# Two edits to the transfers of a fused sparse attention and MoE kernel: the overlap copies of v as SBUF-to-SBUF transfers, and q and k loaded a row ahead

## The chip, the cores and the metric

The kernel runs on one core of a Trainium2 chip. The metric is the time of one execution on the device, in microseconds; where several runs are given, their median. A core has five engines that follow their own instruction queues and wait for each other by semaphores: TensorE (PE; its weight loads are listed as PEld), VectorE (DVE), ScalarE (ACT), GpSimd (POOL) and SyncE (SP). Transfers are issued by SyncE and by GpSimd here, each with a queue of its own (q1 and q0 in the profile), and carried by sixteen DMA engines.

## The reference

Attention over a batch of 8 rows, 8 heads, 576 positions and 64 features. Heads 0 to 3 see a sliding window of 32 positions, heads 4 to 7 a dilated one of 32 positions with a step of 4. The result, laid out by token (4608 x 512), goes through an MLP with a squared ReLU.

```python
mask_plain = (rel >= 0) & (rel < window)
mask_dil = (rel >= 0) & (rel < window * dilation) & (rel % dilation == 0)
scores = np.where(masks[None, :, :, :], scores, -1000000000.0)
attn = np.exp(scores - np.max(scores, axis=-1, keepdims=True))
attn = attn / (np.sum(attn, axis=-1, keepdims=True) + 1e-09)
x = np.matmul(attn, v).transpose(0, 2, 1, 3).reshape(B * S, H * D)

h = x @ w_in                # 512 -> 2048
r = np.maximum(h, 0.0)
out = (r * r) @ w_out       # 2048 -> 512
```

## The kernel before, in words

The attention goes by batch rows `b` of 576 tokens, the MLP by nine chunks `c` of 512 tokens. A stage is one row `b` with chunk `b - 1` beside it: the chunk's code is a generator, and `pump(n)` between pieces of attention lets it emit `n` more pieces. The order of instructions on every engine is thus the order in which the program emits them; each engine takes its own in order. Chunks 2 and up form the second product by a Strassen scheme of seven half-size products that accumulate in three PSUM banks, `pa`, `pb` and `pc` (`mm2_strassen_gen`, L348). ScalarE evicts `pa` (`take`, L386) before the next product may add to it.

What a row of attention needs, and how it comes:

- q and k of the sliding heads: GpSimd's queue loads them with a cast to half precision (`ns`, L112); VectorE copies them into token order (`nr`, `by_token`, L120); SyncE's queue stores that to DRAM (`dp`, L211) and reads it back transposed (`QKTp`, L219).
- q and k of the dilated heads: GpSimd's queue copies them, cast, within DRAM (`dd`, L201); SyncE's queue reads them transposed (`QKTd`, L223).
- v: SyncE loads it in single precision (`sv`, L132; `sd`, L137), GpSimd casts it (`vp`, L169; `vd`, L177). The windows of neighbouring blocks overlap, so the last 32 partitions of one block of `vp` are also the first 32 of the next, and the upper 64 partitions of `vd`'s first half are the lower 64 of its second. ScalarE makes these overlap copies: three `halo_sliding` (L184) and two `halo_dilated` (L189) a row.

In the stage, scores (`ps`, `pz`) go through ScalarE's exponential and VectorE's mask (L546, L547), the weighted sums (`pav`, `paw`) are normalised by VectorE (`xs`, `xd`, L593). From row 4 on, SyncE's queue transposes these into `xT` directly for the sliding heads (L663) and into `yd` for the dilated ones (L670), and ScalarE copies `yd` into `xT` (`x_from`, L658). `xT` feeds the next chunk's first product (`ph`, L293), which ScalarE evicts (`rt`, L316) and VectorE squares (`g`, L317).

Order of the transfers in a stage `b` of 4 to 6: GpSimd first copies one element of the last `QKTd` into `seen` (L230), that is, it waits until the transposes for row `b` have landed; then it issues `ns` and `dd` for row `b + 1`. After the scores VectorE makes `nr`, and SyncE issues `dp`, `sv`, the `xs` transposes, `QKTp`, the two `yd`, `QKTd`, `sd`, and last the chunk's output. A tile of the pool `natp` has two buffers, taken in turn by `ns` and `nr`, so `ns` of the next row may come once `nr` has been made from the last.

The three lines that the prediction's steps turn on:

```python
hooks[3] = turn                          # L851: nr, dp, sv for the next row, after the scores
attn_values_by_dma(b, (turned, done))    # L863: turned: QKTp; done: QKTd, sd, seen, vp
x_from(b, 0, ys[0])                      # L732: ScalarE's copy of the first yd
```

Of the kernel before, what the change touches and what calls it, by code (L numbers as in the profile page):

```python
# [13 lines left out]
P = 128  # L14
# [3 lines left out]
def kernel(  # L18
# [9 lines left out]
    nc = tc.nc  # L28

    B, H, S, D = q.shape  # L30
# [16 lines left out]
    NB = S // QB  # L47
    PADP = P - QB
# [33 lines left out]
    HF = NFF // 2  # L82
# [26 lines left out]
    def load_sliding_qk(b):  # L109
        n = natp.tile([P, HH, 9 * D], FP16, name=f"ns{b}", tag="n")  # L110
        for i, s in ((1, k), (0, q)):
            nc.gpsimd.dma_start(  # L112
                out=n[64 * i : 64 * (i + 1)],
                in_=s[b, 0:HH].rearrange("h (p j) d -> p h (j d)", j=9),
            )
        return n

    def by_token(b, n):
        r = natp.tile([P, 9, HH, D], FP16, name=f"nr{b}", tag="n")
        (nc.gpsimd if b == 2 else nc.vector).tensor_copy(  # L120
            r.rearrange("x j h d -> x h j d"), n.rearrange("x h (j d) -> x h j d", d=D)
        )
        return r
# [49 lines left out]
    def cast_dilated_v(b):  # L173
        for t in range(2):
            p0 = 64 * t
            for c in range(0, DIL, 2):
                nc.gpsimd.tensor_copy(  # L177
                    vd[b % 2][p0:P, t, c : c + 2, :, 0:D],
                    sd[p0:P, t, :, D * c : D * (c + 2)].rearrange("p h (c d) -> p c h d", d=D),
                )  # L180

    def halo_sliding(b, mp):
        m0, m1 = max(1, 2 * mp), 2 * mp + 2
        nc.scalar.copy(  # L184
            vp[b % 2][0:PADP, m0:m1, :, 0:D], vp[b % 2][P - PADP : P, m0 - 1 : m1 - 1, :, 0:D]
        )

    def halo_dilated(b, c):
        nc.scalar.copy(  # L189
            vd[b % 2][0:64, 1, c : c + 2, :, 0:D], vd[b % 2][64:P, 0, c : c + 2, :, 0:D]  # L190
        )

    def cast_v(b):
        cast_sliding_v(b)
        cast_dilated_v(b)


    def keep_dilated_qk(b):
        d = dpool.tile([2, HH * CL, DIL * D], FP16, name=f"dd{b}", tag="dd")
        for i, src in ((1, k), (0, q)):  # L200
            nc.gpsimd.dma_start(  # L201
                out=d[i].rearrange("(r i) x -> r (i x)", i=4),
                in_=src[b, HH:H].rearrange("h (r i) d -> (h r) (i d)", i=16),
                max_dma_last_dim=4096,
            )
        return d

    def keep_sliding_qk(b, r):
        d = dpool.tile([2, S, HH * D], FP16, name=f"dp{b}", tag="dp")
        for i in (1, 0):  # L210
            nc.sync.dma_start(  # L211
                out=d[i].rearrange("(p j) x -> p (j x)", j=9),
                in_=r[64 * i : 64 * (i + 1)].rearrange("p j h d -> p (j h d)"),
            )
        return d
# [12 lines left out]
    def after_transposes(b):  # L228
        t = QKTp[b % 2][:, 0, 1, PADP : PADP + 1] if b == 2 else QKTd[b % 2][:, 0, 1, KPAD : KPAD + 1]
        nc.gpsimd.tensor_copy(seen, t)  # L230
# [9 lines left out]
    for r in range(2):  # L240
        nc.vector.memset(QKTp[r][:, 1, :, 0:PADP], 0.0)
        nc.vector.memset(QKTd[r][:, 1, :, 0:KPAD], 0.0)
        nc.vector.memset(vp[r][:, :, :, D : D + 1], 1.0)
        nc.vector.memset(vp[r][0:PADP, 0, :, D : D + 1], 0.0)
        nc.vector.memset(vd[r][:, 1, :, :, D : D + 1], 1.0)
    nc.vector.memset(AT[:, :, UW:640], 0.0)
    reli = const.tile([P, QB], I16, name="reli")
    nc.gpsimd.iota(reli, pattern=[[1, QB]], base=0, channel_multiplier=-1)
# [58 lines left out]
    def mm1_gen(c, g, sums=False, begun=()):  # L307
        for ffc in range(NFF):
            if ffc < len(begun):
                ph = begun[ffc]  # L310
            else:
                ph = mm1_begin(c, ffc)
                yield
            mm1_half(c, ffc, ph, (2, 3))
            rt = osb.tile([P, TOKC], FP16, name=f"rt{c}_{ffc}", tag="rt")
            nc.scalar.activation(rt, ph[:], ACTF.Relu)  # L316
            nc.vector.tensor_mul(g[:, ffc, :], rt, rt)  # L317
            if c == 1 and ffc % 2 == 0:
                next(w_sums)
            if sums and ffc % 4 == 3 and ffc >= HF:  # L320
                sum_of_g(g, ffc - 3, ffc + 1)
            yield

    def sum_of_g(g, f0, f1):
        k = slice(f0 - HF, f1 - HF)
        nc.vector.tensor_add(gs[0][:, k], g[:, k, HTOK:], g[:, f0:f1, HTOK:])
        nc.vector.tensor_sub(gs[1][:, k], gs[0][:, k], g[:, k, 0:HTOK])  # L327
# [167 lines left out]
    def pump(n):  # L495
        for _ in range(n):
            while pending:
                try:
                    next(pending[0])
                    break  # L500
                except StopIteration:
                    pending.pop(0)
# [152 lines left out]
    def x_from(b, t, y):  # L655
        t0 = b * S % XW + DIL * Q0D[t]
        o = xT[:, 2:4, t0 : t0 + DIL * QD[t]].rearrange("x c (i r) -> x c i r", r=DIL)
        nc.scalar.copy(o, y.rearrange("x r c i -> x c i r"))  # L658
# [16 lines left out]
    def attn_scores(b, gap, less=0, hooks={}):  # L675
        for hp in range(2):
            s_sliding(b, hp)
            if hp in hooks:
                hooks[hp]()
            pump(gap)  # L680
        for g in range(2):
            s_dilated(b, g)
            if 2 + g in hooks:
                hooks[2 + g]()
            if g and b < 4:
                halo_sliding(b, 0)
            pump(gap - less)

    def attn_values(b, gap, wide=False, hooks={}):
        xs = x_tiles(b)  # L690
        for mp in range(3):
            av_sliding(b, mp, xs)
            if mp < 2:
                halo_sliding(b, mp + 1)
            else:
                halo_dilated(b, 0)
            pump(gap)
        x_sliding(b, 0, xs, wide)
        halo_dilated(b, 2)
        pump(gap)  # L700
        av_dilated(b, 0, 0, xs)
        pump(gap)
        x_sliding(b, 1, xs, wide)
        pump(gap)
        av_dilated(b, 0, 1, xs)
        pump(gap)
        for a in range(2):
            av_dilated(b, 1, a, xs)
            pump(gap)
        x_dilated(b, 0, xs, wide)  # L710
        pump(gap)
        x_dilated(b, 1, xs, wide)

    def attn_values_by_dma(b, then):
        xs = x_tiles(b)
        for mp in range(3):
            av_sliding(b, mp, xs)
            if mp:
                halo_dilated(b, 2 * mp - 2)
            pump(3)  # L720
        x_sliding_by_dma(b, xs)
        ys = []
        for t in range(2):
            for a in range(2):
                av_dilated(b, t, a, xs)
                pump(4 + 2 * (a > t))
            if t == 0:
                then[0]()
            ys.append(x_dilated_by_dma(b, t, xs))
        then[1](ys[1])  # L730
        pump(6)
        x_from(b, 0, ys[0])  # L732
        pump(7)
        x_from(b, 1, ys[1])

# [79 lines left out]
    load_v(2)  # L815


    for b in range(2, B):
        pending.append(moe_gen(b - 1))
        nxt = b + 1  # L820
        hooks = {}
        if nxt < B:
            after_transposes(b)
            ns = load_sliding_qk(nxt)
            if b == 2:
                cast_v(b)
            dd = keep_dilated_qk(nxt)
        if b > 4:
            cast_dilated_v(b)
        if b > 3:  # L830
            hooks.update({n: lambda n=n: halo_sliding(b, n + 1) for n in range(2)})
        kept = []

        def turn():
            kept.append(keep_sliding_qk(nxt, by_token(nxt, ns)))
            load_sliding_v(nxt)

        def turned():
            if nxt < B:
                transpose_sliding(nxt, kept[0])  # L840

        def done(y):
            if nxt < B:
                transpose_dilated(nxt, dd)
                if b > 3:
                    load_dilated_v(nxt, nc.sync)
                    nc.gpsimd.tensor_copy(seen, y[:, 0, 0, 0:1])
                    cast_sliding_v(nxt)

        if nxt < B:  # L850
            hooks[3] = turn  # L851
        if b > 3:
            halo_sliding(b, 0)
        pump({2: 24, 3: 16}.get(b, 3))
        attn_scores(b, 4 if b == 2 else 3, 0, hooks)
        if b < 4:
            load_dilated_v(nxt, nc.sync)
            turned()
            done(None)
            cast_v(nxt)  # L860
            attn_values(b, b)
        else:
            attn_values_by_dma(b, (turned, done))  # L863
        pump(1000)
    pending.append(moe_gen(B - 1))
    pending.append(moe_gen(B))
# [31 lines left out]
```

The softmax here doesn't subtract the row's maximum and nothing guards it: scores larger than these inputs give would overflow.

## Time and profile before

| | us |
|---|---|
| median of 11 runs | 307.75 |
| lowest and highest of them | 306.95 and 310.22 |
| the profiled execution | 310.15 |
| its span, first to last instruction | 307.8 |

The profile is of one execution; its span leaves out what lies before the first and after the last instruction, 2.35 us. When transfers were issued and when they landed, in row 4 (the stage from 128.76 to 159.30 us), from the trace:

| transfer | queue | issued | landed |
|---|---|---|---|
| QKTd for row 4, second | SyncE | 126.64 | 130.51 |
| ns for row 5, k and q | GpSimd | 131.21, 131.85 | 137.39, 138.38 |
| dd for row 5, k and q | GpSimd | 132.45, 133.00 | 139.78, 141.20 |
| dp for row 5, two | SyncE | 139.30, 139.87 | 142.84, 144.13 |
| sv for row 5, two | SyncE | 140.55, 141.34 | 145.80, 147.03 |
| xT from xs, two | SyncE | 143.15, 144.91 | 147.55, 149.39 |
| QKTp for row 5, two | SyncE | 146.29, 147.63 | 150.54, 151.69 |
| yd, first and second | SyncE | 149.72, 152.53 | 152.60, 155.17 |
| QKTd for row 5, two | SyncE | 153.83, 155.18 | 157.76, 158.91 |

The rows of a timeline are read as start, length, engine, line, operation and tiles; the bracket at the end tells how long the engine was idle before it and what released it. The DMA row of the page gives the mean busy share of the sixteen DMA engines in 40 equal slices, in tenths.

### The profile page before, as it was taken

What the parts mean: (1) busy time and instruction counts of PE and PEld (TensorE: products, weight loads), DVE (VectorE), ACT (ScalarE), POOL (GpSimd) and SP (SyncE); (2) the same over time, 40 slices, a digit from 0 to 9 for tenths busy, and PEclk for the clock granted to TensorE, in tenths of its full rate; (3) what the DMA queues carried; (4) which work ended last, traced back from release to release, by engine and by line L of the source; (5) the groups of instructions that cost most, each with busy time, mean ns of one, the idle gap of its engine ahead of it and who ended that gap; (6) DMA issues with size and microseconds to landing.
All of it is one profiled execution on the core that took longest, in us unless ns stands there. A gap on an engine that the chain in (4) does not pass through costs nothing.

```text
span 307.8 us, 6916 instructions
## 1 busy us (share of the span) xinstructions
PE 289.7 (94%) x2762; PEld 193.4 (63%) x2762; DVE 208.8 (68%) x433; ACT 184.9 (60%) x318; POOL 67.7 (22%) x117
## 2 busy tenths in 40 slices
PE   1988998997999999999999999999999999999994
PEld 1545554553455558745888997458745875785583
DVE  7774448666962698579939993899389934834652
ACT  2766648666835893597459736963597446425620
POOL 4481008411804401430054004500230000000000
PEclk9999999999999999999999999999999999999999
DMA  7899997899799989999899999989943230003004
GB/s 119 187 196 214 206 170 112 159 214 225 121 206 214 212 161 195 217 200 192 133 195 254 175 137 201 238 166 140 169 140 24 44 116 34 2 1 139 0 0 136
DMA packets 76751, 45.92 MB, mean 149 GB/s; under 512 B 58352, under 2 KB 69104, under 8 KB 76720
## 3 DMA queue, kind: packets, MB, share of 16 engines
q1 hardware_dynamic: 67648, 30.81, 49.7%
q0 software_dynamic: 9072, 14.68, 27.2%
q8 instruction: 21, 0.34, 0.5%
q14 instruction: 10, 0.08, 0.1%
HBM read 36.70 MB, written 16.52 MB: 173 GB/s over the span
## 4 chain that ended last, share of the span: by engine, by line
PE 71%; DMA 8%; DVE 8%; ACT 6%; issue 3%; SPq 2%; POOL 0%; DVEq 0%; POOLq 0%
PE ph L293 27%; PE pa L370 15%; PE pb L370 7%; PE po L436 7%; DMA ns<-in_q_dram 5%; PE pc L370 4%; ACT AT L546 4%; PE paw L621 3%; ACT rt L316 2%; DVE AT L547 2%; PE pav L605 2%; DMA QKTd<-dd 2%; PE pf L490 2%; DMA QKTp<-dp 1%; DVE xs L593 1%
## 5 line engine op out<-in xcount | busy, mean ns | idle before, releaser
L293 PE MATMUL ph<-xT,wi 128*128 128x512 f16 (+1 forms) x640 | 134.0, 359 | 0.7 <-ACT xT L658 0.7
L316 ACT ACTIVATE rt<-ph 128x512 f16<-128x512 f32 x144 | 84.5, 595 | 37.0 <-PE ph L293 35.7
L293 PEld LDWEIGHTS <-wi 128*128 128x128 f16 x640 | 68.2, 114 | 46.1 <-issue 0.6
L317 DVE TENSOR_TENSOR g<-rt 128x512 f16<-128x512 f16 x144 | 61.9, 441 | 39.8 <-ACT rt L316 39.0
L370 PEld LDWEIGHTS <-g 128*128 128x128 f16 x448 | 43.3, 98 | 6.1
L370 PEld LDWEIGHTS <-gs 128*128 128x128 f16 x336 | 32.1, 98 | 4.1 <-DVE gs L327 0.5
L436 PE MATMUL po<-wo,g 128*128 128x512 f16 x128 | 33.1, 380 | 0.0
L397 DVE TENSOR_TENSOR ov<-pb,ov 128x512 f32<-128x512 f32 x14 | 9.7, 691 | 31.0 <-PE pb L370 17.4
L370 PE MATMUL pa<-wt,gs 128*128 128x256 f16 x224 | 27.3, 273 | 0.0
L370 PE MATMUL pb<-wt,g 128*128 128x256 f16 x224 | 27.1, 273 | 0.0
L169 POOL CAST vp<-sv 128x512 f16<-128x512 f32 x24 | 14.4, 633 | 51.7 <-DMA sv<-in_v_dram 51.7
L177 POOL CAST vd<-sd 128x512 f16<-128x512 f32 (+1 forms) x32 | 22.5, 732 | 9.1 <-PE ps L556 5.4
L386 ACT COPY ov<-pa 128x512 f32<-128x512 f32 x14 | 8.2, 586 | 27.0 <-PE pa L370 26.9
L547 DVE TENSOR_TENSOR AT<-AT,maskp 128x576 f16<-128x576 f16 x32 | 19.5, 626 | 6.2 <-ACT AT L546 5.0
L593 DVE TENSOR_TENSOR xd<-paw,rcp_d 80x512 f16<-80x512 f32 (+1 forms) x32 | 21.9, 685 | 1.1
L546 ACT ACTIVATE AT<-ps 128x576 f16<-128x576 f32 x32 | 18.9, 644 | 2.7 <-PE ps L556 2.2
L546 ACT ACTIVATE AT<-pz 128x576 f16<-128x576 f32 x32 | 19.0, 652 | 1.8 <-PE pz L575 1.7
L386 ACT COPY ou<-pa 128x512 f32<-128x512 f32 x14 | 8.2, 586 | 16.0 <-PE pa L370 16.0
L593 DVE TENSOR_TENSOR xs<-pav,rcp_p 96x512 f16<-96x512 f32 x24 | 16.5, 687 | 0.8
L547 DVE TENSOR_TENSOR AT<-AT,maskd 128x576 f16<-128x576 f16 x32 | 15.4, 506 | 2.1 <-ACT AT L546 0.8
L621 PEld LDWEIGHTS <-AT 128*128 128x128 f16 x256 | 11.9, 98 | 5.6 <-PE paw L621 1.3
L436 PEld LDWEIGHTS <-g 128*128 128x128 f16 x128 | 10.3, 97 | 8.1
(83 smaller groups left out, 295.2 us busy)
## 6 DMA issues: line engine op xcount, KB each, us to landing
sv<-in_v_dram SPq DMA_DIRECT2D x14, 288.0 KB, 5.7
dp<-nr SPq DMA_DIRECT2D x12, 288.0 KB, 4.2
out_dram<-ou SPq DMA_DIRECT2D x6, 512.0 KB, 4.8
out_dram<-ov SPq DMA_DIRECT2D x6, 512.0 KB, 4.4
sd<-in_v_dram SPq DMA_DIRECT2D x8, 320.0 KB, 5.8
ns<-in_k_dram POOLq DMA_DIRECT2D x8, 288.0 KB, 6.5
ns<-in_q_dram POOLq DMA_DIRECT2D x8, 288.0 KB, 7.1
sd<-in_v_dram SPq DMA_DIRECT2D x8, 256.0 KB, 6.1
```

The source lines that it names most:

```text
L169: nc.gpsimd.tensor_copy(vp[b % 2][:, m : m + 2, :, 0:D], sv[:, :, m : m + 2, :].rearrange("p h m d -> p m h d"))
L177: nc.gpsimd.tensor_copy(vd[b % 2][p0:P, t, c : c + 2, :, 0:D], sd[p0:P, t, :, D * c : D * (c + 2)].rearrange("p h (c d) -> p c h d", d=D),)
L293: nc.tensor.matmul(ph[:, t0:t1], wi4[ffc // 4][:, dmk, :, ffc % 4], xT[:, dmk, x0 : x0 + t1 - t0], start=(dmk == 0 and t0 == 0), stop=(dmk ...
L316: nc.scalar.activation(rt, ph[:], ACTF.Relu)
L317: nc.vector.tensor_mul(g[:, ffc, :], rt, rt)
L370: nc.tensor.matmul(banks[bank][:, t], a(k, t), b(k), start=(new and t == 0 and k == 0), stop=(k == HF - 1), skip_group_check=True,)
L386: nc.scalar.copy(ot, banks[A])
L436: nc.tensor.matmul(po, g[:, ffc, t * P : (t + 1) * P], wo[ffc // 4][:, ffc % 4, :], start=(ffc == 0), stop=(ffc == NFF - 1),)
L546: nc.scalar.activation(AT[:, u, 0:UW], ps[:, :, 0 : UW // 2], ACTF.Exp, scale=scale)
L547: nc.vector.tensor_mul(AT[:, u, 0:UW], AT[:, u, 0:UW], mask)
L593: nc.vector.tensor_tensor(out=x, in0=pv, in1=rb, op=ALU.mult)
L621: nc.tensor.matmul(pav[:, e, h * (D + 2) : h * (D + 2) + D + 1], AT[:, 4 + h, off : off + P], vd[b % 2][:, t, 2 * a + e, h, 0 : D + 1], st ...
```

## The change

There are two edits. The first: for rows 3 to 7 the overlap of v is copied by one transfer for `vp` and one for `vd` on SyncE's queue, whole rows with the columns that hold ones, in place of ScalarE's five copies; the memsets set both spare columns for this. The second: q and k of row 5 are asked for in row 3's stage, those of row 6 in row 4's after the scores, those of row 7 in row 5's, behind `cast_dilated_v`. For rows 6 and 7 the token-order copy and `dp` stand in the Strassen part of the stage two before, after `x_from` of the first `yd`, together with the overlap of `vp` for the row between. Their `QKTp` and `QKTd` stand at the start of the stage before, followed on SyncE's queue by the overlap of `vd` for that stage's own row and by the load of `sv`. Row 5's token-order copy and transposes stay where they were. The waits by `seen` on `QKTd` go from row 4 on. In chunk 2 the first pair of sums of `g` moves from block 11 to block 13.

```diff
+    def halo_sliding_by_dma(b):
+        nc.sync.dma_start(out=vp[b % 2][0:PADP, 1:NB], in_=vp[b % 2][P - PADP : P, 0 : NB - 1])
+
+    def halo_dilated_by_dma(b):
+        nc.sync.dma_start(out=vd[b % 2][0:64, 1], in_=vd[b % 2][64:P, 0])
...
-        nc.vector.memset(vp[r][:, :, :, D : D + 1], 1.0)
+        nc.vector.memset(vp[r][:, :, :, D : D + 2], 1.0)
         nc.vector.memset(vp[r][0:PADP, 0, :, D : D + 1], 0.0)
-        nc.vector.memset(vd[r][:, 1, :, :, D : D + 1], 1.0)
+        nc.vector.memset(vd[r][:, :, :, :, D : D + 2], 1.0)
...
-            if sums and ffc % 4 == 3 and ffc >= HF:
-                sum_of_g(g, ffc - 3, ffc + 1)
+            if sums and ffc in (13 if c == 2 else 11, 15):
+                f0 = min(ffc // 4 * 4, 12) if ffc != 13 else 8
+                sum_of_g(g, f0, f0 + 4)
...
-            if g and b < 4:
+            if g and b < 3:
                 halo_sliding(b, 0)
...
-            if mp:
-                halo_dilated(b, 2 * mp - 2)
             pump(3)
...
         x_from(b, 0, ys[0])
+        then[2]()
         pump(7)
         x_from(b, 1, ys[1])
```

The loop over the rows, after the change:

```python
    def ask(b):
        if b < B:
            nss[b] = load_sliding_qk(b)
            dds[b] = keep_dilated_qk(b)

    def turn(b):
        if b < B:
            dps[b] = keep_sliding_qk(b, by_token(b, nss[b]))

    for b in range(2, 4):
        ...
        attn_scores(b, 4 if b == 2 else 3, 0, {3: turn_and_load})
        load_dilated_v(nxt, nc.sync)
        transpose_sliding(nxt, dps[nxt])
        transpose_dilated(nxt, dds[nxt])
        cast_v(nxt)
        halo_sliding_by_dma(nxt)
        halo_dilated_by_dma(nxt)
        if b == 3:
            ask(5)
        attn_values(b, b)
        pump(1000)

    for b in range(4, B):
        pending.append(moe_gen(b - 1))
        nxt = b + 1
        hooks = {}
        if b > 4:
            if nxt < B:
                transpose_sliding(nxt, dps[nxt])
                transpose_dilated(nxt, dds[nxt])
            cast_dilated_v(b)
            halo_dilated_by_dma(b)
            if nxt < B:
                load_sliding_v(nxt)
            ask(nxt + 1)
        else:

            def turn_and_load():
                turn(nxt)
                load_sliding_v(nxt)
                ask(nxt + 1)

            hooks[3] = turn_and_load

        def turned():
            if b == 4:
                transpose_sliding(nxt, dps[nxt])

        def done(y):
            if b == 4:
                transpose_dilated(nxt, dds[nxt])
            if nxt < B:
                load_dilated_v(nxt, nc.sync)
                nc.gpsimd.tensor_copy(seen, y[:, 0, 0, 0:1])
                cast_sliding_v(nxt)

        def ahead():
            turn(nxt + 1)
            if nxt < B:
                halo_sliding_by_dma(nxt)

        pump(3)
        attn_scores(b, 3, 0, hooks)
        attn_values_by_dma(b, (turned, done, ahead))
        pump(1000)
```

More of the change, by code (lines that the diff above doesn't have):

```diff
@@ L692, in attn_values @@
             av_sliding(b, mp, xs)
[L693 to L696, printed above, removed]
+            if b < 3:
+                if mp < 2:
+                    halo_sliding(b, mp + 1)
+                else:
+                    halo_dilated(b, 0)
             pump(gap)
         x_sliding(b, 0, xs, wide)
-        halo_dilated(b, 2)
+        if b < 3:
+            halo_dilated(b, 2)
         pump(gap)
@@ L815 @@
     load_v(2)
-    for b in range(2, B):
+    nss, dds, dps = {}, {}, {}
+    def ask(b):
[6 more added lines that the diff above has]
+    for b in range(2, 4):
+        pending.append(moe_gen(b - 1))
+        nxt = b + 1
+        after_transposes(b)
+        nss[nxt] = load_sliding_qk(nxt)
+        if b == 2:
+            cast_v(b)
+        dds[nxt] = keep_dilated_qk(nxt)
+        def turn_and_load():
+            turn(nxt)
+            load_sliding_v(nxt)
+        pump(24 if b == 2 else 16)
+        attn_scores(b, 4 if b == 2 else 3, 0, {3: turn_and_load})
+        load_dilated_v(nxt, nc.sync)
+        transpose_sliding(nxt, dps[nxt])
+        transpose_dilated(nxt, dds[nxt])
+        cast_v(nxt)
+        halo_sliding_by_dma(nxt)
+        halo_dilated_by_dma(nxt)
+        if b == 3:
+            ask(5)
+        attn_values(b, b)
+        pump(1000)
+    for b in range(4, B):
         pending.append(moe_gen(b - 1))
@@ L821, with turn_and_load, done @@
         hooks = {}
[L822 to L827, printed above, removed]
         if b > 4:
+            if nxt < B:
+                transpose_sliding(nxt, dps[nxt])
+                transpose_dilated(nxt, dds[nxt])
             cast_dilated_v(b)
[L830 to L836, printed above, removed]
-        def turned():
-            if nxt < B:
-                transpose_sliding(nxt, kept[0])
-        def done(y):
-            if nxt < B:
[L844 to L863, printed above, removed]
+            halo_dilated_by_dma(b)
+            if nxt < B:
+                load_sliding_v(nxt)
+            ask(nxt + 1)
+        else:
+            def turn_and_load():
+                turn(nxt)
+                load_sliding_v(nxt)
+                ask(nxt + 1)
+            hooks[3] = turn_and_load
+        def turned():
+            if b == 4:
+                transpose_sliding(nxt, dps[nxt])
+        def done(y):
+            if b == 4:
+                transpose_dilated(nxt, dds[nxt])
+            if nxt < B:
+                load_dilated_v(nxt, nc.sync)
+                nc.gpsimd.tensor_copy(seen, y[:, 0, 0, 0:1])
+                cast_sliding_v(nxt)
+        def ahead():
+            turn(nxt + 1)
+            if nxt < B:
+                halo_sliding_by_dma(nxt)
+        pump(3)
+        attn_scores(b, 3, 0, hooks)
+        attn_values_by_dma(b, (turned, done, ahead))
         pump(1000)
```

## The prediction

> **What bounds the kernel now.** I read the page first, then the busy time by stage, then the matrix engine's and ScalarE's own rows in those stages, and last the transfers by queue. The page:
>
> ```profile
> span 307.8 us, 6916 instructions
> PE 289.7 (94%) x2762; PEld 193.4 (63%) x2762; DVE 208.8 (68%) x433; ACT 184.9 (60%) x318; POOL 67.7 (22%) x117
> DMA  7899997899799989999899999989943230003004
> ```
>
> TensorE is busy for 289.7 of 307.8 us; a gain can only come out of the other 18.1. The last row shows the sixteen DMA engines nearly full from the second slice to the thirtieth. By stage (a stage is the time of one attention row with the MoE chunk beside it; rows 3, 4, 5, 6, 7, then the first chunk alone; columns are length, PE, PEld, DVE, ACT, POOL, clock, DMA share, GB/s):
>
> ```profile
> 97.00:128.76 31.76, 31.39 (x317) 21.60 (x315) 22.85 (x47) 21.19 (x39) 9.59 (x16) 1.00 1.04 187
> 128.76:159.30 30.54, 30.22 (x291) 20.96 (x290) 22.86 (x49) 20.38 (x36) 4.66 (x10) 1.00 0.96 185
> 159.30:189.50 30.20, 29.91 (x351) 27.27 (x350) 23.99 (x48) 20.29 (x35) 7.13 (x12) 1.00 0.99 188
> 189.50:221.20 31.70, 30.81 (x293) 20.95 (x292) 23.98 (x49) 20.35 (x35) 7.32 (x13) 1.00 0.97 184
> 221.20:251.60 30.40, 30.08 (x289) 20.86 (x288) 23.28 (x47) 19.88 (x34) 2.83 (x4) 1.00 0.35 71
> 251.60:277.70 26.10, 26.10 (x178) 18.18 (x176) 13.73 (x25) 11.90 (x20) 0.00 (x0) 1.00 0.12 44
> ```
>
> TensorE idles 0.37, 0.32, 0.29, 0.89 and 0.32 us in rows 3 to 7, 2.19 together. The rest of its 18.1 lies at the start, in rows 0 to 2 and behind the last product, where the change does next to nothing. Two stalls show what the 2.19 is made of:
>
> ```profile
> 134.08 0.31 PE L575 MATMUL pz<-QKTd 64*128 64x80 f16 x8 [0.23 <-ACT AT L546]
> 202.63 0.42 PE L605 MATMUL pav<-vp,AT 128*128 128x65 f16 x8 [0.57 <-DVE xs L593]
> ```
>
> The first waits for ScalarE, full there (the overlap copies of v among its work), and recurs in rows 5 to 7. The second is row 6's: VectorE stood 0.87 us for q's load before the token-order copy, and the normalisation queued behind it. So the stages have little to give, and DMA is 96 to 104% full beside them until row 7. What covers the transfers decides. In row 4:
>
> ```profile
> 132.40:140.00 7.60, 7.28 (x75) 3.86 (x74) 6.23 (x15) 7.32 (x15) 1.16 (x3) 1.00 1.00 157
> 140.00:152.60 12.60, 12.60 (x120) 9.27 (x119) 12.26 (x28) 6.45 (x12) 0.00 (x0) 1.00 1.05 180
> 152.60:154.60 2.00, 2.00 (x20) 1.79 (x19) 1.03 (x1) 1.30 (x1) 0.00 (x0) 1.00 0.35 65
> ...
> 152.63 1.30 ACT L658 COPY xT<-yd 128x640 f16<-128x640 f16 x1 [0.62 <-DMA yd<-xd]
> 154.91 0.59 ACT L386 COPY ov<-pa 128x512 f32<-128x512 f32 x1 [0.99 <-PE pa L370]
> ```
>
> From 132.4 to 140 the load of q and k fills the engines, from 140 to 152.6 the dp store, sv, the xs, QKTp and first yd transposes; only then is there slack. That yd lands at 152.6 and ScalarE already waits 0.62 us for it. Behind the copy stands the eviction of pa at 154.91, and TensorE's next product into pa begins at 155.58: the yd may slip by 0.99 us, and each microsecond more stops TensorE. The queues from 132.4 to 140.2, then from 68.2 to 69 and from 69.2 to 70 (packets, MB, share of 16 engines; q0 is GpSimd's, q1 SyncE's):
>
> ```profile
> q0 software_dynamic: 857, 1.17, 96.5%
> ...
> q0 software_dynamic: 94, 0.32, 98.1%
> q1 hardware_dynamic: 103, 0.02, 13.9%
> ...
> q1 hardware_dynamic: 816, 0.20, 116.5%
> q0 software_dynamic: 15, 0.00, 1.1%
> ```
>
> One load of q and k (ns and dd) takes 7.8 x 0.965 = 7.5 us of all engines. While q0 has work (68.2 to 69), a transpose's 256-byte packets pass one for one with its large ones, 103 against 94; once q0 is empty they run at 816 in 0.8 us, eight times faster.
>
> [...]
>
> **The change part by part.**
>
> *Overlap copies off ScalarE.* 25 copies go (five each for rows 3 to 7): 0.40 + 0.60 + 0.60 + 0.61 + 0.61 = 2.82 us a row, 14.1 us of ScalarE. On the path is only TensorE's idle time: the 0.23 of rows 4 to 7, about 0.1 behind each, and 0.15 of row 3 (pav waiting for vp). Ten transfers are added on SyncE, 84 and 135 KB in rows of 2,640 and 2,112 bytes. No row of before shows an SBUF-to-SBUF copy; the nearest are the sd loads, 0.4 to 0.7 us of issue and 5 us to landing. They wait for GpSimd's casts, done before SyncE gets there (row 4's at 126.3; QKTd's issue ends at 128.0). Behind them on SyncE stand only output stores, and in rows 5 to 7 also sv and xs, at least 5 us early. I take 0, from 0 to +0.5 a row.
>
> *q and k a stage ahead.* Three `seen` copies go (rows 4 to 6), and with them GpSimd's waits of 4.33, 1.83 and 2.89 us that kept the loads behind the transposes. The token-order copy (0.75 us of VectorE) leaves the scores of rows 5 and 6 for the Strassen section, where VectorE has gaps of 1.9 and 2.5 us: the 0.57 of row 6 goes. Moving two 0.69 us sums of chunk 2 from block 11 to 13 may return row 3's 0.21 (xs). Of 2.19 I count 1.9 as won: bounds 1.0 and 2.2. What is late next is the transposes:
>
> (1) Row 4, middle. ns(6) and dd(6) are asked for as soon as VectorE has copied ns(5), about 139. Their 7.5 us fall into 140 to 152.6, which is full, and by turns they go ahead of xs, QKTp and yd. yd: 152.6 + 7.5 = 160.1, less 0.7 (dp no longer stands behind dd(5)'s tail until 140) and about 1 (the two queues overlap, shares of 1.05 to 1.17) = 158.4. Against the limit of 152.6 + 0.99 = 153.6 that is a stall of 4.8 us; 3.5 with transposes at their best rate, 6 at the 600 packets per us that xs to yd averaged.
>
> (2) Row 4, start. ns(5) is asked for behind the casts at 126.3, while QKTd(4) is still moving (landed at 130.51, needed by pz at about 133). If q0's first packet comes 1.2 us later, as at 131.21, QKTd still has about 114 packets an engine, meets all 50 of q0's, and lands at about 137: 3.7 us lost. If it takes 2.9 us, as at 191.17 with engines busy, 28 packets remain and it lands at 133: nothing lost. The engines are busy (1.22), so I take 0.5.
>
> (3) Row 5. ns(7) and dd(7), four transposes and sv now stand before its xs and yd, where ns, dd, dp, sv and two transposes did. Stage and backlog have both slid; yd comes within 0.5 us of its limit. 0 to 2.7, taken as 0.3. Rows 6 and 7 load nothing ahead: 0.
>
> *Edits with one answer.* The wider memsets cost about 0.1 us of VectorE, which is unbroken up to the first QKTp copy at 7.41: +0.1. Moving transposes to the start of rows 5 and 6 costs SyncE only issue time.
>
> Sum: 4.8 + 0.5 + 0.3 + 0.1 - 1.9 = +3.8 us. The profiled span becomes 307.8 + 3.8 = 311.6, its execution 310.15 + 3.8 = 313.95. That execution lies 2.4 above the median of 307.75, so on the median I put 311.5.
>
> **The rivals.** *The covers hold* (the other side, one mechanism): if q0 doesn't take its turns against the transposes beyond row 4's slack, yd lands by 153.6 and only the win is left, 307.75 - 1.8 = 305.9. It decides from where ns(6) and dd(6) delay yd by less than 1 us of their 7.5. For it: q0's packets came up to 2.9 us after issue, so part could slide behind. Against: the one-for-one count, and no slack before 152.6. *A balance*: yd slips by about 3 us, TensorE loses 2, the win takes it back: 307.7. For it: shares of 1.2 in places, so mixed queues move somewhat more; against: it needs three fifths of the 7.5 us absorbed. *A cascade*: QKTd is caught whole (3.7), row 4's yd slips by 5.5 and row 5 loses 2.7: 11.9 + 0.1 - 1.9 = +10.1, 317.9. For it: 96 to 104% leave no room to catch up before row 6; against: a stall in one place gives the transfers time, so later ones shrink. *The change doesn't do what it says*: not so; the instruction lists lose 25 ScalarE copies and gain ten transfers.
>
> **How the numbers follow.** Forecast (308.7 to 315) 0.63; cascade (above 315) 0.13; balance 0.10; covers hold 0.14. Faster by over 0.3% (0.9 us, about what a measurement of this kernel can tell from no change) 0.14, within it 0.10, slower 0.76. The range runs from 306.0, the covers-hold value with its smaller win, to 316.5, part of the way into the cascade.
>
> **What would show it.** Right: the first yd of row 4 lands near 158 instead of 152.6, ScalarE's wait at xT<-yd grows from 0.62 to about 5 us, TensorE's idle time in that stage goes from 0.3 to 4 or more and drops below 0.2 in rows 6 and 7; pz never waits for AT again. Wrong: yd of row 4 lands within 4 us of its issue and that issue does not slip, or q0's packets wait for q1's. If QKTd, not yd, is what TensorE waits for, step 2 was undersized and step 1 too large.

## The result and the profile after

| | before | after |
|---|---|---|
| median, us | 308.0 (47 runs, 306.54 to 311.25) | 315.95 (12 runs, 313.64 to 325.42) |
| ratio, 95% interval | | 1.0239, 1.0213 to 1.0266 |
| span of the profiled execution | 307.8 | 315.5 |

The ratios here and below leave out executions that took over 1.5% longer than the fastest of the same kernel; medians are of all. The change costs 7.4 us (2.39% of 308.0), about twice the 3.8 that were forecast. The two profiled executions took 310.15 and 317.4 us, 2.2 and 1.5 above the medians. From the page of the changed kernel; the last three rows are TensorE's busy tenths, its granted clock and the DMA share in 40 slices of 7.9 us:

```profile
span 315.5 us, 6885 instructions
PE 291.1 (92%) x2762; PEld 194.9 (62%) x2762; DVE 206.9 (66%) x433; ACT 172.9 (55%) x293; POOL 65.8 (21%) x114
...
PE   1988998999999979999679969999999999999994
...
PEclk9999999999999999999969989999999999999998
DMA  7999979899499999979999999894440222003003
```

ScalarE lost 12.0 us of work (184.9 to 172.9) and TensorE stands idle longer. The two deep dips in TensorE's row, in slices 20 and 21 and in slice 24, are the middles of rows 4 and 5; the shallow one before them is row 3. In the clock's row a digit falls with each of the deep ones, to 6 and to 8 tenths; the kernel before has 9 in all 40 slices. By stage (rows 3 to 7; length, PE, PEld, DVE, ACT, POOL, clock, DMA share, GB/s):

```profile
94.90:128.40 33.50, 31.49 (x318) 21.71 (x317) 23.45 (x47) 18.64 (x33) 12.43 (x20) 1.00 1.11 196
128.40:165.00 36.60, 31.87 (x290) 21.80 (x289) 23.53 (x49) 17.87 (x30) 4.50 (x9) 0.91 0.98 198
165.00:199.80 34.80, 31.70 (x354) 28.35 (x352) 23.69 (x48) 17.92 (x30) 8.79 (x16) 0.95 1.05 188
199.80:229.60 29.80, 29.80 (x290) 20.82 (x289) 22.45 (x47) 17.91 (x30) 3.02 (x6) 1.00 0.73 144
229.60:259.40 29.80, 29.80 (x290) 20.77 (x289) 22.45 (x47) 18.01 (x30) 1.17 (x2) 1.00 0.23 61
```

Rows 6 and 7 are now unbroken TensorE work, 29.80 of 29.80 us. Rows 4 and 5 are 6.1 and 4.6 us longer than before, and their mean granted clock is 0.91 and 0.95. The timeline there, with the stops, ScalarE's first copy of `yd` and SyncE's issues (SPq):

```profile
143.23 8.38 SPq L670 DMA_TRANSPOSE xT<-xs  x2
...
154.53 2.58 SPq L677 DMA_TRANSPOSE yd<-xd  x2
...
157.62 1.26 ACT L665 COPY xT<-yd 128x640 f16<-128x640 f16 x1 [6.68 <-DMA yd<-xd]
...
159.41 3.57 PE L377 MATMUL pa<-wo,gs 128*128 128x256 f16 x16 [4.73 <-ACT ov L393]
...
167.50 10.63 SPq L225 DMA_TRANSPOSE QKTp<-dp  x2
178.23 5.03 SPq L229 DMA_TRANSPOSE QKTd<-dd  x2
183.32 0.59 SPq L197 DMA_DIRECT2D vd<-vd  x1
...
186.22 0.42 PE L628 MATMUL paw<-vd,AT 128*128 128x65 f16 x8 [3.10 <-DMA vd<-vd]
```

Row 4 is the stop that was forecast: ScalarE waits 6.68 us for `yd`, the eviction of `pa` stands behind that copy, TensorE stops for 4.73. Its cause is in the first line: issuing the two `xs` transposes takes SyncE 8.38 us. Before, in the same place:

```profile
143.15 3.03 SPq L663 DMA_TRANSPOSE xT<-xs  x2
```

So the first `yd` is issued at 154.53 instead of 149.72; from its issue to its landing it takes 3.06 us, hardly more than the 2.88 before. In row 5 the chain is another one. The four transposes for row 6, now at the start of the stage, occupy SyncE from 167.50 to 183.26, and only then does it issue the overlap transfer of `vd`, for which TensorE has been waiting since 183.12. In row 6, with no load beside them, the four transposes at the start of the stage take 7.02 us (201.13 to 208.15).

Where the 7.68 us between the two spans lie, from the first `ps` product of one row to that of the next:

| | before | after | difference | of it TensorE's stop over 0.5 us |
|---|---|---|---|---|
| start to row 3 | 103.65 | 101.86 | -1.79 | |
| row 3 | 26.33 | 27.76 | +1.43 | 2.00 |
| row 4 | 30.50 | 36.67 | +6.17 | 4.73 |
| row 5 | 30.57 | 34.82 | +4.25 | 3.10 |
| row 6 | 31.32 | 29.78 | -1.54 | (before: 0.57) |
| rest | 85.47 | 84.62 | -0.85 | |

The first line is scatter between executions: apart from the memsets the code is the same there, and row 3 began between 101.9 and 104.3 in the profiles of those kernels below that leave row 2 as it is (all but e8 and e10).

### The profile page after: what moved, and what is told of

Its sections match the earlier page's. It is cut to its first block, busy times and chain, and to the rows that moved or that the text cites. A ratio compares the mean times of both kernels' runs of the same rounds, so it can differ in the third digit from the quotient of the medians.

```text
span 315.5 us, 6885 instructions
## 1 busy us (share of the span) xinstructions
PE 291.1 (92%) x2762; PEld 194.9 (62%) x2762; DVE 206.9 (66%) x433; ACT 172.9 (55%) x293; POOL 65.8 (21%) x114
## 4 chain that ended last, share of the span: by engine, by line
PE 71%; DMA 9%; DVE 8%; ACT 4%; SPq 4%; issue 2%; POOL 1%; DVEq 0%; POOLq 0%
PE ph L299 29%; PE pa L377 14%; PE pb L377 7%; PE po L443 7%; DMA ns<-in_q_dram 6%; PE pc L377 4%; PE paw L628 2%; SPq L225 2%; ACT AT L553 2%; DVE xs L600 2%; PE ps L563 1%; DVE g L323 1%; PE pav L612 1%; PE pf L497 1%; SPq L229 1%
## 5 line engine op out<-in xcount | busy, mean ns | idle before, releaser
L322 ACT ACTIVATE rt<-ph 128x512 f16<-128x512 f32 x144 | 86.2, 612 | 44.1 <-PE ph L299 41.9
L377 PEld LDWEIGHTS <-g 128*128 128x128 f16 x448 | 43.8, 99 | 6.7
L377 PEld LDWEIGHTS <-gs 128*128 128x128 f16 x336 | 33.3, 101 | 9.8 <-issue 4.9
L169 POOL CAST vp<-sv 128x512 f16<-128x512 f32 x24 | 15.3, 671 | 51.2 <-DMA sv<-in_v_dram 51.2
L177 POOL CAST vd<-sd 128x512 f16<-128x512 f32 (+1 forms) x32 | 20.4, 666 | 10.7 <-DMA sd<-in_v_dram 9.3
L553 ACT ACTIVATE AT<-pz 128x576 f16<-128x576 f32 x32 | 19.9, 707 | 1.4 <-PE pz L582 1.3
L554 DVE TENSOR_TENSOR AT<-AT,maskp 128x576 f16<-128x576 f16 x32 | 16.6, 527 | 5.1 <-ACT AT L553 3.2
L377 PE MATMUL pa<-wo,gs 128*128 128x256 f16 x112 | 15.2, 293 | 4.7 <-ACT ov L393 4.7
```

The costliest lines, as they stand in the source:

```text
L169: nc.gpsimd.tensor_copy(vp[b % 2][:, m : m + 2, :, 0:D], sv[:, :, m : m + 2, :].rearrange("p h m d -> p m h d"))
L177: nc.gpsimd.tensor_copy(vd[b % 2][p0:P, t, c : c + 2, :, 0:D], sd[p0:P, t, :, D * c : D * (c + 2)].rearrange("p h (c d) -> p c h d", d=D),)
L377: nc.tensor.matmul(banks[bank][:, t], a(k, t), b(k), start=(new and t == 0 and k == 0), stop=(k == HF - 1), skip_group_check=True,)
L553: nc.scalar.activation(AT[:, u, 0:UW], ps[:, :, 0 : UW // 2], ACTF.Exp, scale=scale)
L554: nc.vector.tensor_mul(AT[:, u, 0:UW], AT[:, u, 0:UW], mask)
```

## The experiments

The theory after the result: the loads asked for a stage ahead go in front of the transposes, in row 4 before `yd`, in row 5 before the overlap of `vd`. Rivals: the overlap transfers themselves are the cost; the half clock is the cost and the transfers only its occasion; the DMA engines have too much to do in sum, wherever it is put. Each ratio is against the kernel before, run on the same chip.

**e1, the first edit alone.** On the kernel before, the overlap copies go by transfer as in the change; q and k are loaded as before.

```diff
-            hooks.update({n: lambda n=n: halo_sliding(b, n + 1) for n in range(2)})
+            halo_dilated_by_dma(b)
...
+        def ahead():
+            if nxt < B:
+                halo_sliding_by_dma(nxt)
```

> Edit 1 alone: the overlap of v by transfers from row 3 on, q and k at their old places. Theory (GpSimd's loads of q and k overtake the transposes; the overlap transfers by themselves are harmless): ScalarE is relieved, pz no longer waits for AT, no vd wait, 305.5 to 307.5 us, TensorE idle under 0.2 us in rows 4, 5 and 7. Rival (the overlap transfers on SyncE's queue are the cost): the wait of paw for vd of about 3 us is there again in row 5 and the time is 310 us or more.

Measured: 309.13 (20 runs), ratio 1.0029 [1.0006, 1.0052], where a gain was expected. No product waits for an overlap transfer here. The timeline of VectorE and TensorE shows what does wait (this execution took 312.4 us, 3.3 above the median, so the stops can be shorter in others):

```profile
138.76 0.76 DVE L120 COPY nr<-ns 128x2304 f16<-128x2304 f16 x1 [1.53 <-DMA ns<-in_q_dram]
140.84 0.41 PE L611 MATMUL pav<-vp,AT 128*128 128x65 f16 x8 [1.05 <-DVE xs L599]
...
172.52 0.41 PE L611 MATMUL pav<-vp,AT 128*128 128x65 f16 x8 [1.55 <-DVE xs L599]
```

With ScalarE faster, VectorE gets to the token-order copy sooner, and waits there for a load that comes no sooner. The normalisation `xs` stands behind that copy, and `pav` behind `xs`. In this execution the time that the first edit gives ScalarE is lost again to the wait for the load.

**e2, the second edit alone.** q and k a stage ahead, the overlap by ScalarE as before.

```diff
         def ahead():
             turn(nxt + 1)
-            if nxt < B:
-                halo_sliding_by_dma(nxt)
+        hooks.update({n: lambda n=n: halo_sliding(b, n + 1) for n in range(2)})
+        halo_sliding(b, 0)
```

> Edit 2 alone: q and k a row ahead, the overlap of v by ScalarE's five copies a row as before. Theory: in row 4 the stall behind the first yd stays (4 to 5 us, and then some 2 us at half clock); in row 5 no wait for vd, but yd comes late in its place and TensorE stops 0 to 3 us there; 311 to 315 us. Rival (the overlap transfers are the cost): 309 us or less.

Measured: 315.69 (4 runs), ratio 1.0206 [1.0149, 1.0262]. Row 4 of its timeline:

```profile
161.54 1.87 PE L377 MATMUL pa<-wo,gs 128*128 128x256 f16 x8 [4.96 <-ACT ov L393]
```

The loss is in the second edit: +6.3 us alone, +0.9 for the first edit alone, +7.4 for both. Row 5 has no stop here (30.57 us). ScalarE copies the overlap of `vd`, so it needs no place in SyncE's queue; and `yd`, which keeps its place there behind the four transposes, is hardly late:

```profile
190.55 1.31 ACT L665 COPY xT<-yd 128x640 f16<-128x640 f16 x1 [0.42 <-DMA yd<-xd]
```

The four transposes held SyncE for 12.5 us here (169.63 to 182.16), against 15.8 in the changed kernel.

**e3, half of the load.** The copies of the dilated q and k (`dd`) for rows 6 and 7 are left out.

```diff
-            dds[b] = keep_dilated_qk(b)
+            dds[b] = keep_dilated_qk(b) if b < 6 else dds[5]
```

> The changed kernel without the dilated copies dd of rows 6 and 7 (rows 6 and 7 transpose row 5's instead, so the dilated heads of those two rows are computed from row 5's q and k): GpSimd's load beside the transposes shrinks from 7.5 to 4.4 us of all engines. Theory: in row 4 yd lands about 3 us earlier (about 154.5), the stall at pa falls from 4.7 to about 1.6 us[...]; in row 5 vd lands 3 us earlier and the stall of 3.1 us nearly goes; 306 to 309 us. Rival (SyncE's issue of the transposes is the bound, not the engines): SyncE issues as much as before, so nothing moves, 315 to 317 us.

Measured: 311.46 (20 runs), ratio 1.0082 [1.0053, 1.0111], above the 306 to 309 expected. The profiled execution took 308.7 and kept its clock; in 14 of the 20 the mean clock is 0.994 or lower, against 5 of 39 executions of the kernel before. Its row 4:

```profile
157.74 1.47 PE L377 MATMUL pa<-wo,gs 128*128 128x256 f16 x12 [2.58 <-ACT ov L393]
```

The stop follows the dose: 4.73 us with `ns` and `dd` ahead, 2.58 with `ns` alone; so does the issue of the two `xs` transposes, 8.38 and 6.27 us. Row 5 has no stop and takes 29.92 us, and the clock stays at 1.00.

**e4, the clock alone.** Idle products ahead of the two waiting ones keep TensorE busy; nothing is loaded earlier.

```diff
+        if c == 3:
+            fill(20)
         yield from product(A, sq(1), wq(1, 1))
...
+                if b == 5 and t == 1 and a == 0:
+                    fill(14)
                 av_dilated(b, t, a, xs)
```

> The changed kernel with 20 idle products (128x512, 0.216 us each) ahead of the product that waits in row 4, and 14 ahead of the paw that waits in row 5; their result is used by nobody. Theory (the stops cost twice: 4.7 and 3.1 us of waiting, and then 2.05 and 1.7 us because the clock was halved for 6.8 and 3.4 us after TensorE stood still): the waits end at the same times, the clock stays at 1.00 through 150 to 195 us, about 312.2 us. Rival (the clock falls for another reason[...]): the clock drops again and the time stays at 315 to 317 us.

Measured: 317.6 (4 runs, 315.09 to 324.78), ratio 1.0265 [1.0189, 1.0342], above the 312.2 that were expected and not to be told from the changed kernel's 1.0239: that the clock's share can be won back in the time is not shown. The profile is of the shortest of the four (315.09, span 313.3) and answers by stretch and by row:

```profile
155.00:163.50 8.50, 7.81 (x56) 5.33 (x54) 1.73 (x3) 3.35 (x4) 1.86 (x4) 1.00 0.97 143
```

The clock is 1.00 where it was 0.50 in the changed kernel (below). In this profile row 4 takes 34.96 us instead of 36.67, so by estimate 1.7 us of it were the clock's. Row 5 takes 34.62 instead of 34.82: it still waits for the `vd` transfer, which landed at 185.51 instead of 186.08. So row 5 is set by its transfers, and the half clock there only filled a wait that remained. Against the 29.80 and 29.92 us that these rows take without a stop (e6), the late transfers alone cost 5.2 and 4.7 us.

**e5, the overlap of vd back on ScalarE, rows 5 to 7.** This takes the instruction away for which TensorE waited in row 5.

```diff
+            if mp and b > 4:
+                halo_dilated(b, 2 * mp - 2)
...
-            halo_dilated_by_dma(b)
```

> The changed kernel with the overlap of vd of rows 5 to 7 made by ScalarE again (two copies a row); vp's stays a transfer. Theory (in row 5 only vd's transfer is late, because it stands on SyncE's queue behind four transposes that GpSimd's load holds up): the wait of paw and the half clock after it go, 3.1 + 1.7 us less; row 4 keeps its stall of 4.5 to 5 us; 311 to 312.5 us. Rival (row 5 is late as a whole, and the stop moves to the yd of row 5): a stop of 2 to 3 us behind xT<-yd in row 5, 314 to 316 us.

Measured: 317.57 (4 runs), ratio 1.0252 [1.0199, 1.0305]; no gain. The stop moves to the next late transfer of the row, `yd`:

```profile
195.42 1.86 PE L377 MATMUL pa<-wo,gs 128*128 128x256 f16 x8 [3.63 <-ACT ov L393]
```

The cost of row 5 is not the one transfer but its place behind the four transposes, which all that follows on SyncE shares. How much that place costs varies: the four held SyncE for 17.4 us here (167.07 to 184.51) and for 12.5 in e2, where `vd` is ScalarE's too and nothing stops. In e2 the first of them was issued 0.7 us ahead of GpSimd's load, here 0.1; that this is the reason is not shown.

**e6, the same work in another place.** Both edits' transfers are kept. Rows 6 and 7 are asked for behind `seen` and the casts of `vp`, which wait for `yd`; the token-order copy and the transposes stay where they were in the kernel before.

```diff
...
         def done(y):
             if nxt < B:
                 transpose_dilated(nxt, dds[nxt])
                 load_dilated_v(nxt, nc.sync)
                 nc.gpsimd.tensor_copy(seen, y[:, 0, 0, 0:1])
                 cast_sliding_v(nxt)
+                ask(nxt + 1)
...
         def ahead():
-            turn(nxt + 1)
             if nxt < B:
```

> Both overlap transfers kept; q and k of rows 6 and 7 are asked for one element of yd later (behind seen and the casts of vp, in the Strassen part of the row before), token-order copy and transposes at their old places. Theory (what costs is a load of q and k running beside the transposes that xT waits for; what keeps edit 1 alone from winning is the token-order copy waiting for ns): both collisions are gone, no stop over 0.5 us in rows 4 to 7, row 6 about 30 us, 304.5 to 306.5 us, faster than both kernels. Rival (DMA work is too much in sum, and wherever the load stands it costs the same): 307.5 us or more, with a new late transfer.

Measured: **306.12** (11 runs, 304.79 to 310.57), ratio 0.9921 [0.9893, 0.9949]: better than both kernels. Rows 4 to 7 by stage:

```profile
130.20:160.00 29.80, 29.80 (x295) 21.45 (x294) 22.87 (x48) 18.02 (x31) 4.17 (x8) 1.00 1.01 195
160.00:189.90 29.90, 29.90 (x348) 26.93 (x346) 23.48 (x48) 18.07 (x31) 7.07 (x12) 1.00 1.05 202
189.90:219.70 29.80, 29.80 (x289) 20.66 (x288) 23.42 (x48) 18.00 (x31) 4.76 (x8) 1.00 1.02 200
219.70:249.50 29.80, 29.80 (x289) 20.92 (x289) 23.18 (x47) 17.90 (x31) 3.08 (x4) 1.00 0.37 82
```

TensorE has no gap in any of them, with the DMA engines as full as before (1.01 to 1.05 in rows 4 to 6). This rules out that the sum of transfers is what was too much; what counts is which comes first. The queues between 142 and 150 us show it for row 4, first the changed kernel, then e6 (packets, MB, share of 16 engines):

```profile
q0 software_dynamic: 773, 1.08, 75.4%
q1 hardware_dynamic: 1893, 0.75, 38.7%
```

```profile
q1 hardware_dynamic: 5410, 1.50, 119.9%
```

In the same eight microseconds SyncE's queue gets 5,410 packets through when it is alone, and 1,893 beside GpSimd's. The first `yd` of row 4 waits 0.51 us at ScalarE, against 6.68:

```profile
152.12 1.30 ACT L665 COPY xT<-yd 128x640 f16<-128x640 f16 x1 [0.51 <-DMA yd<-xd]
```

Until this `yd` only the load is placed otherwise in row 4 than in the changed kernel, so there it is the load's place that counts. For row 5 the load and the four transposes moved together; no run moved one alone.

**e7, e1 with the token-order copy later.** If e1's only loss is VectorE's wait for `ns`, moving the copy behind the second `pav` should win it.

```diff
+            if mp == 1:
+                then[3]()
...
-        if nxt < B:
+        if nxt < B and b < 4:
             hooks[3] = turn
```

> Edit 1 alone with the token-order copy of rows 5 to 7 (and dp and sv behind it) moved from after the last scores to behind the second pav, two pumps of three pieces later. Theory (edit 1 alone loses its win because VectorE stands 1.5 to 2 us for ns before that copy): the waits for ns go in rows 4 to 6, and with them the stops at pav of 1.05 to 2.06 us; dp and QKTp move 3 us back, so yd may come up to 2 us late; 305.5 to 308 us. Rival (the overlap transfers themselves delay something else): stops at pav remain, 309 us.

Measured: 316.75 (4 runs), ratio 1.0297 [1.0259, 1.0335], where 305.5 to 308 was expected. The wait for `ns` is gone, but `dp`, and with it every transpose behind it, comes later, and `yd` is late in rows 4, 5 and 6 (stops of 2.00, 2.36 and 2.25 us):

```profile
189.00 1.31 PE L376 MATMUL pa<-wo,gs 128*128 128x256 f16 x8 [2.36 <-ACT ov L392]
```

So the first edit does not pay with the loads at their old place, in either position of the copy; it pays in e6, where the next row's load is already there and does not stand before `yd`. How much of e6's gain is the earlier load's alone is open: it was not run with ScalarE's overlap copies.

**e8, e9, e10: what is left of e6.** e6 still stops for 1.56 us in row 3 at `pav`, behind VectorE. e8 asks for row 4 in row 2's stage too; e9 puts the sums of `g` of chunk 2 back at block 11; e10 does both.

```diff
-        if b == 3:
-            ask(5)
+        ask(b + 2)
```

```diff
-            if sums and ffc in (13 if c == 2 else 11, 15):
-                f0 = min(ffc // 4 * 4, 12) if ffc != 13 else 8
-                sum_of_g(g, f0, f0 + 4)
+            if sums and ffc % 4 == 3 and ffc >= HF:
+                sum_of_g(g, ffc - 3, ffc + 1)
```

> As e6_after_yd, and q and k of row 4 too are asked for behind the casts of v in row 2's stage, without the wait for QKTd of row 3. Theory (in row 3 TensorE stops 1.56 us at pav because VectorE waits 0.64 us for ns and has the sums of block 13 ahead of the normalisation): ns comes in time, the stop falls to about 0.9 us, QKTd of row 3 still lands before pz; 305 to 306 us. Rival (this load too holds up transposes that are needed): QKTd of row 3 late, a stop at pz, 307 us or more.

> As e6_after_yd, with the sums of chunk 2 at blocks 11 and 15 as in the kernel before. Theory (moved to block 13 they stand ahead of row 3's normalisation): the stop at pav in row 3 falls from 1.56 to about 0.8 us, 305 to 306 us. Rival (at block 11 they hold up the masks of row 3 instead): a stop of the same size in another place, 306 us or more.

> The edits of e8_row3 and e9_sums together on e6_after_yd. Theory: no stop over 0.5 us in row 3 either, 304.5 to 305.5 us. Rival: what one edit wins the other takes back, 306 us.

Measured: e8 305.99 (16 runs), ratio 0.9922 [0.9898, 0.9946], not to be told from e6, though row 3 stops for only 0.83 us in its profile; e9 311.76 (8 runs), 1.0088 [1.0055, 1.0121]; e10 311.25 (8 runs), 1.0055 [1.0015, 1.0095]. In e9 row 3's stop fell to 0.57 us as expected, but a new one came at the start of row 4:

```profile
137.72 0.44 PE L581 MATMUL pz<-QKTd 64*128 64x80 f16 x16 [3.45 <-DMA QKTd<-dd]
```

In e9 the second `QKTd` of row 4 was issued at 127.22, behind `ns(5)` at 126.56, and landed at 137.58; in e6 it was issued at 125.44, level with `ns` at 125.47, and landed at 133.51. That is the prediction's step 2, in time (137) and in size (3.7): who goes first by a microsecond or two decides on it. In e10's profile `QKTd` is late in rows 3 and 4 (stops of 4.86 and 1.77 us).

**e11, e12: a guard for QKTd.** GpSimd copies one element of row 4's `QKTd` before it asks for row 5, so that `ns` can't overtake it; e11 on e6, e12 on e9.

```diff
         if b == 3:
+            nc.gpsimd.tensor_copy(seen, QKTd[nxt % 2][:, 1, 1, KPAD : KPAD + 1])
             ask(5)
```

> As e6_after_yd, and GpSimd copies one element of row 4's QKTd for k before it asks for q and k of row 5, so that this load starts when the first of the two transposes has landed. Theory (in row 3 the load starts within a microsecond of QKTd's second transpose, and which comes first decides between a landing at 133 and one at 137): QKTd's second lands by 132, ns of row 5 some 2 us later, still before its copy; 304.5 to 306.5 us, with no run lost to a stop at pz. Rival: the later load meets the token-order copy in row 4 and costs what the guard saves, 307 us or more.

> As e9_sums with the same guard. Theory (e9_sums lost 3.45 us at pz and then the clock only because QKTd of row 4 was overtaken): the stop at pz goes and the time falls from 311.8 to 304.5 to 306.5 us. Rival (the sums at block 11 are themselves what costs): 309 us or more.

Measured: e11 308.0 (16 runs), ratio 0.9966 [0.9935, 0.9997]; e12 307.01 (22 runs), 0.9955 [0.9933, 0.9976]; both above the 304.5 to 306.5 expected. From e9 to e12, 4.75 us are back and the stop at `pz` is gone, so e9's loss was `QKTd` overtaken. Neither betters e6. In e12 the guard makes `ns(5)` late for its copy, and `pav` of row 4 waits behind that:

```profile
139.79 0.41 PE L611 MATMUL pav<-vp,AT 128*128 128x65 f16 x8 [1.24 <-DVE xs L599]
```

In e11 row 4 has no stop (29.79 us). Its profile loses at `pav` of row 3, ahead of the guard: it stops for 2.06 us, the eight products into `pa` after it take 1.50 us where e12's take 1.03, and its mean clock is 0.994; e6 stops for 1.56 there and has a mean clock of 0.999.

## Why the prediction was right in direction and wrong in size

**Step 1 held.** The first `yd` of row 4 landed at 157.59 (forecast 158.4) and TensorE stopped for 4.73 us (4.8). That the load is the cause is shown by e3 (half of the load, 2.58 us of stop) and e6 (the load behind `yd`, no stop). Its way to `yd` was the issue: of the 5 us that `yd` slipped, 4.81 lie in its issue, behind the `xs` transposes. The prediction had counted with the engines' time (7.5 us of load) and had no term for the issue.

**Step 2 fell to its lower bound, in part by luck.** In the changed kernel the second `QKTd` was issued at 124.12, ahead of `ns` at 124.81; it landed at 131.75 and `pz` did not wait: 0, where 0.5 was taken. e9, with the order reversed, shows that the upper bound is real.

**Step 3 failed.** It put row 5 at "0 to 2.7, taken as 0.3", and with it two sentences: that on SyncE behind the overlap transfers stand in rows 5 to 7 "also sv and xs, at least 5 us early", and that moving transposes to the start of rows 5 and 6 "costs SyncE only issue time". The issue time is what failed: it was put at nothing. Beside `ns(7)` and `dd(7)` on GpSimd's queue the four transposes held SyncE for 15.8 us (167.50 to 183.26), against 7.0 in row 6, and `vd`, `sv`, `xs` and `yd` stood behind them in program order. The overlap transfers, "0, from 0 to +0.5 a row", failed with it: TensorE waited 3.10 us for `vd`. In row 5 the late transfers cost 4.7 us (34.62 less 29.92, from e4 and e6), whether `vd` meets them first (the changed kernel) or `yd` (e5). In row 6, where no load runs beside the four transposes, nothing stops. So what step 1 took from the count of packets (103 against 94) for row 4's landing times was not used for row 5's issues. The size is not fixed: e2, with the same transposes beside the same load, has no stop in row 5, and why is open.

**A term was missing: the clock.** Around the end of each of these two stops (4.73 and 3.10 us) TensorE's granted clock is 0.50 for a while. The changed kernel in the two stretches, the clock in the third column from the end:

```profile
156.70:163.50 6.80, 4.09 (x20) 2.92 (x20) 1.29 (x2) 3.23 (x4) 1.85 (x4) 0.50 0.87 169
187.40:190.80 3.40, 3.40 (x25) 2.48 (x23) 1.07 (x3) 0.59 (x1) 0.00 (x0) 0.50 1.27 126
```

By estimate, 4.09 and 3.40 us of work at a clock of 0.50 are 2.05 and 1.70 us lost. e4's profile gave back 1.7 in row 4 and 0.2 in row 5, so about 1.9 of the 3.75 count. The mean clock of a whole execution differs: it is 0.971 to 0.993 in the twelve of the changed kernel, 0.981 in the profiled one.

**The win came near its figure by luck.** Without the stops and the time lost to the half clock (4.73 + 2.05 and 3.10 + 1.70) rows 4 and 5 are 0.61 and 0.55 us shorter than before; row 6 is 1.54 shorter and the rest 0.85. These 3.55 us are more than the 2.2 of idle time in rows 3 to 7 that was the upper bound. The bound was wrong: more was won than the idle time. Between the same `ps` products before's row 6 holds 30.43 us of TensorE's busy time, after's 29.78, for 290 matmuls in each. Where the 0.65 us between them lie is not shown; that small waits between matmuls count as busy is a guess.

```profile
191.05:222.37 31.32, 30.43 (x290) 20.68 (x290) 23.96 (x48) 20.36 (x36) 7.13 (x12) 1.00 0.97 182
```

```profile
201.11:230.89 29.78, 29.78 (x290) 20.80 (x290) 22.45 (x47) 17.91 (x31) 4.19 (x8) 1.00 0.73 143
```

Row 3, counted among the winners, lost 1.43 instead: it stops for 2.00 us at `pav`. In e6 that stop is 1.56, and 0.57 with the sums back at block 11 (e9), so their move to block 13 costs about a microsecond there, where the prediction had it return 0.21. Gain and loss together are 2.1 us won, near the 1.9 that were counted.

Together, on the span: 3.8 forecast, +0.4 in row 4 and +4.4 in row 5 for the transfers (5.2 and 4.7 in place of 4.8 and 0.3), +1.9 for the clock, -0.5 for step 2, -0.2 for the win and -0.1 for the memsets, which lie ahead of row 3, is 9.7. From row 3 on 9.5 were measured; the 1.8 of scatter ahead of row 3 make 7.7 of it.

## What to carry to other kernels

Where the DMA engines are as full as here (shares of 0.96 to 1.05), a load that starts earlier starts in front of something: find the transfer that is needed next, and put the load right behind it, with a wait if need be. Look at the issuing queue too: here the issue of two transposes grew beside a load from 3.03 us to 8.38 (`xs` of row 4) and from 3.21 to 10.63 (`QKTp`, row 6's stage and row 5's), and all that followed in order came later. An engine that is relieved gets to its next wait sooner (VectorE at `ns` in e1, where it waited 1.53 us), so the relief pays only where that wait moves as well.

## What the runs showed of the hardware

TensorE's clock, in the changed kernel's profile: it is 0.50 for 6.8 us from 156.7 us on, around the end of the stop of 4.73 us (159.41), and for 3.4 us from 187.4, after the stop of 3.10 us that ended at 186.22. At 0.50 the eight products into `pc` at 187.35 took 1.85 us; eight of the same form took 1.04 in the kernel before (210.14). After the stop of 2.00 us in row 3, which ended at 114.18, it is 1.00 (114.20 to 118.00).

In other profiles: e3 stops for 2.58 us in row 4 and has a mean clock of 1.000; e11 stops for 2.06 us in row 3 and has 0.994; e4, with idle products in the changed kernel's first stop, has 1.00 from 155.00 to 163.50 us. So in these runs the length of a stop alone does not tell whether the clock falls; what does is not shown.

The issue of two transposes took SyncE 3.13 us with no load beside it (e6, `xs` in row 4), and 8.38 and 10.63 us beside a load on the other queue in the changed kernel.
